# A new unit order for a one-core Sinkhorn-attention and gMLP kernel: V of the first batch mixed in 128 columns, narrow dummy matmuls ahead of P

## The chip, the core and the metric

The kernel runs on one core of a Trainium2 chip. The metric is device time in microseconds (us) of one execution, as the median of several runs. Before the change the median of five runs is 167.9 us (166.93 to 168.35).

The engines of the core are named as in the profile: PE is TensorE (PEld its weight loads), DVE is VectorE, ACT is ScalarE, POOL is GpSimd and SP is SyncE. Each works through its own instructions in program order, and semaphores order them against each other. DMAs are issued from two of these queues: SP issues the ones that move data between tiles, the transposing ones and the results; POOL issues the loads.

## What is computed

There are 4 batches (B), 8 heads (H), 768 positions (S) and 64 columns per head (D). A position belongs to one of 8 blocks of 96.

```
P = sort_net                                  # B, H, 8, 8
5 times: P = exp(P - rowmax); P /= rowsum; P /= colsum
k_sorted = P mixed over the 8 blocks of k     # and v_sorted likewise
attn     = softmax(q_block @ k_sorted_block.T / 8)   # inside each block of 96
x        = attn @ v_sorted_block              # B, S, 512
h = relu(x @ w_in)                            # 1024 columns: u = first half, v = second half
v_n = layer norm of v over its 512 columns
gated = u * (w_spatial @ v_n + b_spatial)     # w_spatial is 768 x 768
out = gated @ w_out
```

All matmuls take bf16 operands and sum in fp32.

## The kernel before

Its work is cut into units. A unit is a function `u_XY`, and the string `ORDER` is a list of calls, `XY:args`, that is run from first to last. There is no planner at run time: the place of a unit in `ORDER` is the place of each of its instructions on each engine and in each queue that it uses. Where an argument is a letter, it names the engine that empties PSUM or does the elementwise step (A for ACT, D for DVE, P for POOL). Where the first argument is a digit 0 to 7, it is the PSUM bank at which the unit's result starts; most units take two banks, and a unit whose banks are still being read waits on PE.

The units that the change and the prediction speak of:

- `LH`, `L`: one load each, issued by POOL (`L:k:2` loads k of batch 2; `L:wv`, `L:wu`, `L:ws`, `L:wo` the weights). q, k and v have two buffers each, so the load of batch 2 needs the buffer of batch 0.
- `SK`: one of five Sinkhorn rounds (ACT and DVE). `PR`: P spread by 8 small matmuls. `P0`: the mixing matrices of batch 0, in four parts on DVE. `PC`: a copy of the spread P, from which `PD` (POOL) makes the mixing matrices `pd` of the other batches.
- `DM:bank:n:w`: n dummy matmuls on a zeroed tile, w columns wide; nothing reads them.
- `QT`, `KT`: q turned, and k mixed and turned, for one pair of heads: 12 matmuls into two banks and one copy of 128x768. `QX`: for batches 2 and 3, q is turned by a DMA instead: two DVE copies (L180) and a transposing DMA on SP (L182).
- `VT` and `VX`, batch 0 only: v mixed and turned for one pair of heads (L338, then a copy), and turned back by 4 transposes per half of the blocks (L375), into `vb`. `VM` and `VC`, other batches: v mixed without turning (L387), then 4 DMAs per half (L402, SP) that regroup it into `vb`.
- `SC`: scores of one pair of heads and one half of the blocks (8 small matmuls, L420), and their exponential on ACT (`ex`, four buffers). `AT`: 8 small matmuls with `vb` (L445), and the division: on DVE, or, for the letter P, an ACT copy, a DVE reciprocal and a POOL product.
- `XT`: x of batch 0 turned on PE. `XX`: x of half a batch turned by a transposing DMA on SP (L189), for batches 1 to 3.
- `VP`: v half of the first layer, tiles of 128 positions, 4 matmuls of 512 columns each (L488), relu and statistics. `LN`: the reciprocal deviations (ACT). `LA`: normalising one tile (POOL L518 and L519, or DVE L522).
- `UP`: u half, 8 matmuls of 384 columns (L533). `WS`: w_spatial turned, 6 transposes. `BB`: the load of b_spatial.
- `SP`: the spatial product for 128 columns, 12 matmuls of 384 columns (L545), then `z` (DVE) and the gate `gt` (DVE or POOL). `OP`: two output tiles, 8 matmuls of 512 columns (L594), a copy and the store. `SH` and `OH` are their halves at the end of the last batch.
- `WT`: a one-element POOL copy of a tile that a transposing DMA writes. What POOL issues after it waits until that DMA has landed.

In the order before, the turned v of batch 0 is made in halves of 64 columns (8 `VT` units), and each half has a buffer of its own (tag `vT`, three buffers). k and q of batch 3 stand behind `WT:x:1:0`, and `QX:D:3` stands on DVE ahead of `LA:D:1:1` and `LA:D:1:3`.

Of the kernel before, what the change touches and what calls it, by code (L numbers as in the profile page):

```python
# [9 lines left out]
BF16 = mybir.dt.bfloat16  # L10
# [38 lines left out]


# [9 lines left out]
def kernel(  # L60
# [25 lines left out]
    HP = H // 2  # L86
# [7 lines left out]
    att = ctx.enter_context(tc.tile_pool(name="att", bufs=2))  # L94
# [49 lines left out]
    st = {}  # L144
# [190 lines left out]
    def mix_T(t, src, b, hp, lo, n):  # L335
        for g in range(G):
            for hh in range(2):
                nc.tensor.matmul(  # L338
                    t[hh * 64:hh * 64 + 64, g * n:(g + 1) * n],
                    lhsT=src[:, 2 * hp + hh, g * D:(g + 1) * D],  # L340
                    rhs=pd[b][:, 2 * hp + hh, lo:lo + n],
                    start=True, stop=True,
                )
# [12 lines left out]
    def u_VT(ps, eng, hp, ih):  # L356
        hp, ih = int(hp), int(ih)
        lo, n = (0, 128) if ih == 2 else (ih * 64, 64)
        t = ps_tile(ps).rearrange("p x c -> p (x c)")
        mix_T(t, st["v", 0], 0, hp, lo, n)  # L360
        vT = att.tile([128, n * G], BF16, name="vT", tag="vT", bufs=3)
        copy(
            eng,
            vT.rearrange("p (x g) -> p x g", g=G),
            t[:, 0:n * G].rearrange("p (g x) -> p x g", g=G),
        )
        for y in range(2):
            if ih in (y, 2):
                st["vT", hp, y] = vT[:, HW * y if ih == 2 else 0:][:, 0:HW]
# [272 lines left out]
```

## Time and profile before

| | |
|---|---|
| median of 5 runs | 167.9 us (166.93 to 168.35) |
| profiled execution: its time | 168.42 us |
| profiled execution: span, first to last instruction | 166.6 us |
| PE matmuls busy | 142.4 us, 85% of the span |
| DVE / ACT / POOL busy | 117.6 / 82.6 / 52.8 us |
| mean granted TensorE clock | 0.98 |
| mean DMA rate | 153 GB/s, 25.49 MB moved |

The profile is of one execution. The span leaves out 1.8 us of the execution's own time. The strips of the page cut the span into 40 slices of 4.17 us; a digit is the busy share of a slice in tenths, and PEclk is the clock that PE was granted. The list of waits says which engine and line stood idle, what ended the idle time, how many microseconds in all, how often, and the longest one. The chain of waits is followed back from the last instruction; each of its lines has a start, a length and what took the time.

### The profile page before, as it was taken

The page shows a single profiled execution, that of the slowest core. Times are in us where ns is not written, and L with a number is a line of the kernel's source. Part 1 is how long each engine was busy: PE and PEld are TensorE (multiplying, and loading weights), DVE is VectorE, ACT ScalarE, POOL GpSimd, SP SyncE. Part 2 cuts the span into 40 slices and gives each one's busy share as a digit, 9 for nine tenths or more (in the row PEclk, how much of TensorE's full clock was granted, in tenths as well). Part 3 has the DMA queues.
Part 4 walks back from the last instruction along what each step waited for, and adds up shares of the span by engine and source line. Part 5 has one row for each costly group of instructions (what it writes and reads, how often), then busy time and mean ns, then how long its engine had stood idle before and what let it go on. Part 6 is the DMA issues. An engine that isn't in the chain of part 4 may idle for free.

```text
span 166.6 us, 3795 instructions
## 1 busy us (share of the span) xinstructions
PE 142.4 (85%) x1545; PEld 86.9 (52%) x1559; DVE 117.6 (71%) x237; ACT 82.6 (50%) x127; POOL 52.8 (32%) x73
## 2 busy tenths in 40 slices
PE   0477888999999898999973599999999999999790
PEld 0345777565866754555541265654555655456330
DVE  3767868896986859867720864989967897409950
ACT  3323968576984923684881023436762406740011
POOL 7915950249424535162600040032104200200300
PEclk9999999999999999999999569999999999999999
DMA  2999999999999999979999995000383500053055
GB/s 21 160 195 204 207 210 207 204 204 206 203 256 260 201 144 168 213 123 119 241 252 178 263 244 99 0 0 29 114 208 130 94 0 0 35 213 134 0 191 189
DMA packets 36689, 25.49 MB, mean 153 GB/s; under 512 B 16576, under 2 KB 33472, under 8 KB 36672
## 3 DMA queue, kind: packets, MB, share of 16 engines
q0 software_dynamic: 14864, 12.19, 48.3%
q1 hardware_dynamic: 21808, 13.06, 33.0%
q8 instruction: 12, 0.20, 0.5%
q14 instruction: 5, 0.04, 0.1%
HBM read 24.78 MB, written 6.29 MB: 186 GB/s over the span
## 4 chain that ended last, share of the span: by engine, by line
PE 47%; DMA 30%; POOL 7%; DVE 6%; issue 4%; ACT 3%; SPq 1%; POOLq 0%; ACTq 0%; DVEq 0%
DMA v_in<-in_v_dram 15%; PE ps L545 11%; DMA q_in<-in_q_dram 11%; PE ps L488 9%; PE ps L533 8%; PE ps L594 6%; DMA vb<-vm 3%; PE ps L445 3%; PE ps L420 3%; PE ps L338 2%; DVE z L551 2%; POOL v_sb L519 2%; POOL k_in L155 2%; PE ps L375 1%; DMA out_dram<-oh_sb 1%
## 5 line engine op out<-in xcount | busy, mean ns | idle before, releaser
L545 PE MATMUL ps<-wspT,v_sb 128*128 128x384 bf16 x180 | 32.8, 337 | 4.1 <-DVE v_sb L522 4.1
L457 POOL TENSOR_TENSOR x_sb<-xr,rec 96x512 bf16<-96x512 f32 x13 | 13.4, 1039 | 49.4 <-DVE rec L456 49.4
L433 ACT ACTIVATE ex<-ps 96x768 bf16<-96x768 f32 x32 | 24.8, 804 | 7.9 <-PE ps L420 7.4
L545 PEld LDWEIGHTS <-v_sb 128*128 128x128 bf16 x180 | 17.5, 100 | 16.1 <-DVE v_sb L522 4.5
L533 PE MATMUL ps<-xT,w_in_sb 128*128 128x384 bf16 x128 | 23.6, 331 | 0.1
L488 PE MATMUL ps<-w_in_sb,xT 128*128 128x512 bf16 x88 | 21.9, 379 | 0.4
L551 DVE TENSOR_TENSOR z<-ps,b_bc 128x768 f32<-128x768 f32 x15 | 14.2, 954 | 10.8 <-PE ps L545 8.8
L502 DVE BATCH_NORM_STATS2 stats<-v_sb 128x6 f32<-128x512 bf16 x24 | 16.3, 679 | 3.6 <-ACT v_sb L113 3.1
L594 PE MATMUL ps<-w_out_sb,gt 128*128 128x512 bf16 x67 | 16.3, 379 | 0.5 <-issue 0.3
L533 PEld LDWEIGHTS <-w_in_sb 128*128 128x128 bf16 x128 | 12.2, 99 | 8.3 <-issue 0.5
L113 ACT ACTIVATE v_sb<-ps 128x1024 bf16<-128x1024 f32 (+1 forms) x8 | 7.3, 916 | 14.7 <-PE ps L488 10.8
L519 POOL TENSOR_SCALAR v_sb<-v_sb,nm,rstd 128x512 bf16<-128x512 bf16 x11 | 8.8, 796 | 16.7 <-issue 11.2
L453 ACT COPY xr<-ps 96x520 f32<-96x520 f32 x13 | 7.4, 586 | 13.1 <-PE ps L445 11.8
L488 PEld LDWEIGHTS <-xT 128*128 128x128 bf16 x96 | 8.9, 98 | 9.3
L445 PE MATMUL ps<-vb,ex 96*128 96x65 bf16 x256 | 12.7, 196 | 1.1 <-DMA vb<-vm 0.9
L457 DVE TENSOR_TENSOR x_sb<-ps,rec 96x512 bf16<-96x512 f32 x19 | 13.0, 687 | 0.7
L445 PEld LDWEIGHTS <-ex 96*128 96x128 bf16 x256 | 10.9, 99 | 4.3 <-issue 1.6
L113 ACT ACTIVATE u_sb<-ps 128x768 bf16<-128x768 f32 x12 | 9.7, 811 | 6.1 <-PE ps L533 5.8
L557 DVE TENSOR_TENSOR gt<-z,u_sb 128x768 bf16<-128x768 f32 x12 | 12.2, 1014 | 0.4
L323 PE MATMUL ps<-ident,q_in 128*64 128x128 bf16 x96 | 4.6, 243 | 7.7 <-DMA q_in<-in_q_dram 6.4
L107 ACT CAST vm<-ps 128x768 bf16<-128x768 f32 x10 | 7.8, 801 | 6.1 <-PE ps L387 6.0
L594 PEld LDWEIGHTS <-gt 128*128 128x128 bf16 x72 | 6.6, 98 | 7.3
(89 smaller groups left out, 207.0 us busy)
## 6 DMA issues: line engine op xcount, KB each, us to landing
out_dram<-o_sb SPq DMA_DIRECT2D x9, 512.0 KB, 4.2
k_in<-in_k_dram POOLq DMA_DIRECT2D x4, 768.0 KB, 13.8
v_in<-in_v_dram POOLq DMA_DIRECT2D x4, 768.0 KB, 12.1
vb<-vm SPq DMA_DIRECT2D x24, 99.0 KB, 7.5
q_in<-in_q_dram POOLq DMA_DIRECT2D x3, 768.0 KB, 20.1
out_dram<-oh_sb SPq DMA_DIRECT2D x6, 256.0 KB, 2.1
wsp_nat<-in_moe_w_spatial_dram POOLq DMA_DIRECT2D x1, 1152.0 KB, 21.5
w_in_sb<-in_moe_w_in_dram POOLq DMA_DIRECT2D x2, 512.0 KB, 15.9
```

Source lines behind the costliest of these rows:

```text
L113: nc.scalar.activation(out=out, in_=in_, func=AF.Relu)
L433: nc.scalar.activation(out=dst, in_=src, func=AF.Exp, scale=scale)
L445: nc.tensor.matmul(t[:, hh, ii * VW:ii * VW + D + 1], lhsT=e[:, c:c + 128], rhs=vb[b % 2][:, ih * NI + ii, 2 * hp + hh, 0:D + 1], start=Tr ...
L457: (nc.gpsimd if eng == "P" else nc.vector).tensor_mul(out=x_sb[:, hp].rearrange("p i (h d) -> p h i d", h=2), in0=tv[:, :, :, 0:D], in1=_r ...
L488: nc.tensor.matmul(t[:, x, :], lhsT=x_tile(b, n // 3)[:, kc, n % 3 * 128:(n % 3 + 1) * 128], rhs=w_in_sb[:, kc, DH:DFF], start=(kc == 0), ...
L502: nc.vector.bn_stats(out=stats, in_=v_sb[:, x, :])
L519: nc.gpsimd.tensor_scalar(out=v_sb, in0=v_sb, scalar1=nm[:, 0:1], scalar2=rs[:, n:n + 1], op0=ALU.add, op1=ALU.mult)
L533: nc.tensor.matmul(t[:, x, 0:HW], lhsT=w_in_sb[:, kc, mc * 128:(mc + 1) * 128], rhs=x_tile(b, ih)[:, kc], start=(kc == 0), stop=(kc == KC ...
L545: nc.tensor.matmul(t[:, x, 0:HW], lhsT=st["v_sb", b, n][:, mc * 128:(mc + 1) * 128], rhs=wspT[:, n, x * HW:(x + 1) * HW], start=(n == 0), ...
L551: nc.vector.tensor_add(out=z.rearrange("p (x c) -> p x c", x=2), in0=t[:, :, 0:HW], in1=b_bc.rearrange("p (x c) -> p x c", x=2),)
L557: eng.tensor_mul(out=gt, in0=z, in1=st["u", b, mc // 2][:, mc % 2])
L594: nc.tensor.matmul(t[:, x, :], lhsT=st["gt", b, mc][:, c * 128:(c + 1) * 128], rhs=w_out_sb[:, mc, :], start=(mc == 0), stop=(mc == FC - 1),)
```

## The change

Three things change. First, `VT` writes all 128 columns for a pair of heads at once (four units instead of eight), into one tile that holds all four pairs and takes the buffer of tag `qX`, which batches 2 and 3 use later for their turned q. Second, the dummies ahead of `PR` are four groups of 12 with 192 columns and one of 2 with 384, where they were two groups of 6 with 384; two single dummies later on are gone. Third, the whole `ORDER` is another one: other places, banks and engines for nearly all units. The number and kind of the other units is the same.

Parts of the new order that matter for what follows: five `PD` units stand between `L:wv` and `L:v:1`, three of them ahead of `L:ws`; `L:v:1`, `L:k:1`, `L:q:1` stand behind the POOL product of an `AT`; `L:v:3` comes before the attention of batch 1 instead of behind it; k and q of batch 3 stand behind `WT:q:2:0`; on SP, both transposes of x of batch 1 come before the one of q of batch 2, and the regrouping of v of batch 3 (`VC:3`) comes after `QX:D:3`; `QX:D:3` comes after two `SP` units of batch 1.

```diff
--- before.py
+++ after.py
@@ -14,37 +14,37 @@
 
 
 ORDER = """
-LH:q:0:0:4 IN SK:0 ID MK SK:0 SK:0 L:k:0:0:128 QT:0:A:0:1:2 SK:0 QT:2:A:0:0:2 DM:0:6:384 SX
-DM:2:6:384 SK:1 PR:0 L:v:0:0:128 P0:1:0:4 P0:0:0:4 P0:1:4:8 P0:0:4:8 DM:7:5:384 KT:2:D:0:1:2 PC:A
-KT:4:A:0:0:2 KT:0:D:0:2:2 VT:7:A:1:0 VT:6:A:3:0 IV:0 VT:2:D:0:0 LH:q:0:4:8 SC:4:0:0:1 VX:7:D:1:0 L:wv
-SC:0:0:1:0 VX:2:D:3:0 VT:6:D:0:1 L:wu L:ws QT:4:A:0:3:2 IV:1 VT:7:D:2:0 SC:0:0:0:0 VX:6:D:0:1
-AT:2:D:0:1:0 KT:4:A:0:3:2 QT:6:A:0:2:2 PD:1:4:8 VX:0:D:0:0 VX:1:D:2:0 SC:4:0:3:0 AT:2:D:0:0:1
-VT:0:A:1:1 L:v:1:0:128 VT:7:D:3:1 VT:1:A:2:1 AT:4:D:0:3:0 SC:2:0:2:0 AT:6:D:0:0:0 PD:3:4:8 VX:0:A:2:1
-L:k:1:0:128 DM:1:1:384 SC:4:0:1:1 AT:2:D:0:2:0 SC:0:0:2:1 VX:7:D:1:1 XT:6:A:0:0:0 VX:4:D:3:1
-XT:2:D:0:0:1 AT:0:D:0:2:1 SC:3:0:3:1 L:q:1:0:128 AT:6:D:0:1:1 PD:1:0:4 VP:2:A:0:2 PD:3:0:4 L:wo
-PD:2:0:4 AT:3:P:0:3:1 VP:0:D:0:0:1 XT:7:A:0:1:0 UP:3:A:0:0:0 XT:7:A:0:1:1 VM:0:D:1:1 WS:6:D:0
-WS:2:D:3 LN:0:0:3 LA:P:0:1 L:v:2:0:128 WS:3:D:1 VM:4:A:1:3 VP:7:A:0:5 VP:0:A:0:3:4 UP:2:A:0:0:1
-LA:P:0:2 VM:6:A:1:2 UP:0:D:0:1:1 LA:P:0:0 VM:2:A:1:0 VC:1:1 KT:6:D:1:0:2 KT:4:A:1:1:2 KT:0:A:1:3:2 BB
-QT:2:D:1:2:2 QT:6:A:1:0:2 L:k:2:0:128 LN:0:3:6 KT:4:D:1:2:2 QT:0:D:1:3:2 VC:1:0 QT:2:A:1:1:2 LA:D:0:4
-L:q:2:0:128 SC:6:1:0:1 UP:4:D:0:1:0 PD:2:4:8 SC:2:1:2:1 SC:0:1:3:1 WS:7:D:4 WS:6:D:5 VM:4:A:2:2
-LA:P:0:5 VM:2:D:2:3 WS:7:D:2 VM:0:A:2:1 LA:P:0:3 DM:6:1:384 SC:4:1:1:1 AT:2:D:1:0:1 AT:0:P:1:2:1
-SC:6:1:0:0 L:v:3:0:128 AT:4:D:1:1:1 AT:2:D:1:3:1 SP:0:P:0:3 SC:4:1:1:0 KT:6:A:2:0:2 KT:2:D:2:2:2
-SC:4:1:3:0 KT:0:D:2:3:2 AT:6:P:1:1:0 KT:2:D:2:1:2 SC:4:1:2:0 XX:1:1 AT:0:P:1:3:0 QX:D:2 SP:6:D:0:0
-AT:0:P:1:2:0 AT:2:D:1:0:0 XX:1:0 SP:4:P:0:1 VM:6:A:2:0 SP:0:D:0:2 VC:2:1 VM:2:A:3:1 VM:6:A:3:3
-VP:4:D:1:4:5 VM:6:A:3:2 VM:0:A:3:0 UP:2:D:1:0:1 SC:6:2:1:1 LN:1:4:6 SC:0:2:0:1 LA:P:1:4 VC:3:0
-WT:x:1:0 L:k:3:0:128 OP:4:D:0:2 L:q:3:0:128 SC:2:2:3:1 SC:6:2:2:1 UP:0:A:1:1:0 VC:2:0 AT:2:D:2:1:1
-AT:4:P:2:0:1 VP:6:D:1:0:1 AT:4:P:2:2:1 AT:2:P:2:3:1 VP:0:A:1:2:3 SC:2:2:1:0 SC:6:2:2:0 UP:4:A:1:1:1
-VC:3:1 XX:2:1 OP:0:D:0:0 LN:1:0:4 LA:P:1:0 SC:4:2:0:0 SC:6:2:3:0 UP:2:A:1:0:0 KT:0:A:3:2:2 LA:D:1:2
-LA:D:1:5 KT:6:A:3:3:2 QX:D:3 LA:D:1:1 LA:D:1:3 OP:4:D:0:1 AT:0:D:2:3:0 AT:6:P:2:2:0 SP:2:D:1:0
-AT:0:P:2:1:0 AT:4:D:2:0:0 UP:6:A:2:1:1 SP:2:D:1:2 VP:4:A:2:4:5 SC:2:3:2:1 SC:6:3:3:1 SP:0:D:1:3
-AT:2:P:3:2:1 SP:4:D:1:1 XX:2:0 KT:0:D:3:1:2 KT:2:A:3:0:2 UP:6:A:2:1:0 AT:2:D:3:3:1 VP:4:D:2:0:1
-SC:2:3:1:1 LN:2:4:6 LA:P:2:5 SC:6:3:1:0 OP:0:A:1:0 AT:2:D:3:1:1 LA:D:2:4 VP:4:D:2:2:3 SC:2:3:0:1
-SC:0:3:3:0 OP:6:A:1:2 AT:0:D:3:0:1 AT:2:D:3:1:0 LN:2:0:4 UP:4:D:2:0:0 UP:6:A:2:0:1 SC:2:3:2:0
-SC:0:3:0:0 LA:P:2:0 LA:D:2:3 LA:D:2:1 XX:3:1 LA:D:2:2 OP:4:D:1:1 AT:2:P:3:2:0 AT:6:P:3:3:0 SP:0:D:2:2
-AT:6:D:3:0:0 VP:4:A:3:4:5 UP:0:A:3:1:1 LN:3:4:6 SP:2:D:2:1 SP:0:D:2:3 XX:3:0 SP:2:D:2:0 VP:0:A:3:2:3
-VP:2:A:3:0:1 UP:0:A:3:0:0 UP:6:A:3:1:0 LA:D:3:4 LN:3:0:4 LA:D:3:3 LA:P:3:5 OP:0:A:2:0 LA:P:3:0
-LA:D:3:1 UP:6:A:3:0:1 LA:D:3:2 OP:2:A:2:2 OP:6:A:2:1 SP:2:D:3:0 SP:6:D:3:2 SP:2:P:3:1 SH:7:D:3:3:0
-SH:6:D:3:3:1 OH:7:D:3:1 OH:6:D:3:0 OH:2:A:3:4 OH:7:D:3:5 OH:6:D:3:2 OH:2:A:3:3
+IN LH:q:0:0:4 ID SK:0 MK SK:0 SK:0 QT:0:A:0:1:2 QT:2:D:0:0:2 DM:0:12:192 SK:0 L:k:0:0:128 SX
+DM:2:12:192 L:v:0:0:128 SK:1 DM:0:12:192 IV:0 DM:2:12:192 DM:7:2:384 PR:0 P0:1:4:8 P0:0:4:8 P0:1:0:4
+P0:0:0:4 PC:A DM:7:5:384 KT:2:A:0:2:2 KT:4:D:0:3:2 IV:1 KT:0:A:0:1:2 VT:6:D:1:2 KT:2:A:0:0:2
+LH:q:0:4:8 VT:4:D:0:2 SC:0:0:1:1 VX:7:D:1:0 L:wv SC:2:0:0:1 PD:3:4:8 L:wu VX:6:D:1:1 VT:0:D:3:2
+QT:4:A:0:2:2 PD:2:0:4 PD:1:4:8 QT:6:D:0:3:2 L:ws VT:2:A:2:2 PD:3:0:4 PD:2:4:8 VX:0:D:0:1 AT:4:P:0:1:1
+VX:1:D:3:0 SC:6:0:2:0 L:v:1:0:128 SC:2:0:2:1 VX:0:D:2:1 L:k:1:0:128 AT:4:D:0:0:1 VX:1:A:2:0 PD:1:0:4
+SC:6:0:3:1 VX:0:D:0:0 AT:2:D:0:2:1 AT:4:D:0:2:0 VX:1:A:3:1 SC:6:0:3:0 SC:2:0:1:0 L:q:1:0:128
+AT:0:D:0:3:1 AT:6:D:0:3:0 SC:4:0:0:0 AT:2:P:0:1:0 XT:0:A:0:1:1 XT:1:D:0:1:0 AT:6:P:0:0:0 XT:4:A:0:0:1
+WS:2:A:3 WS:3:D:0 VP:0:D:0:3:4 WS:7:A:1 XT:2:A:0:0:0 VP:3:D:0:5 VM:0:A:1:2 VM:6:A:1:3 VM:4:A:1:1
+VP:2:D:0:2 VM:0:A:1:0 LN:0:3:6 VP:6:A:0:0:1 VC:1:0 UP:0:A:0:1:0 KT:6:A:1:2:2 KT:4:A:1:1:2
+KT:2:D:1:3:2 UP:0:D:0:0:1 L:wo LA:P:0:3 LN:0:0:3 L:v:2:0:128 QT:6:A:1:3:2 LA:P:0:5 QT:2:D:1:1:2
+L:k:2:0:128 KT:4:A:1:0:2 QT:0:D:1:0:2 SC:6:1:3:0 WS:2:D:4 L:q:2:0:128 SC:4:1:3:1 LA:P:0:2
+QT:0:D:1:2:2 LA:D:0:4 SC:6:1:1:0 SC:2:1:0:0 WS:4:D:2 WS:5:D:5 L:v:3:0:128 AT:0:D:1:3:0 UP:6:A:0:1:1
+LA:P:0:0 VC:1:1 LA:P:0:1 SC:4:1:2:0 AT:2:D:1:0:0 AT:0:D:1:1:0 UP:6:A:0:0:0 AT:2:D:1:2:0 AT:4:D:1:3:1
+BB SP:0:D:0:3 SC:4:1:2:1 SC:2:1:0:1 SP:6:P:0:1 VM:2:A:2:1 KT:4:D:2:3:2 AT:0:P:1:2:1 XX:1:0 SC:6:1:1:1
+KT:2:A:2:0:2 AT:0:D:1:0:1 SP:4:D:0:2 AT:0:P:1:1:1 VM:2:A:2:2 SP:6:P:0:0 XX:1:1 VM:2:A:2:3 QX:D:2
+VM:4:A:2:0 VP:0:D:1:0:1 UP:4:A:1:0:0 VM:2:D:3:0 VC:2:0 VM:0:A:3:1 OP:6:D:0:2 KT:0:D:2:1:2 WT:q:2:0
+L:k:3:0:128 KT:2:A:2:2:2 VP:4:A:1:2:3 L:q:3:0:128 VM:0:A:3:3 UP:2:A:1:1:1 SC:4:2:3:0 VC:2:1
+SC:6:2:2:0 VP:0:D:1:4:5 SC:4:2:1:0 SC:2:2:0:0 UP:6:A:1:1:0 AT:0:D:2:3:0 LN:1:0:4 LN:1:4:6 LA:D:1:5
+AT:4:P:2:2:0 LA:P:1:2 LA:D:1:1 OP:2:A:0:0 LA:D:1:4 LA:D:1:0 LA:D:1:3 AT:6:P:2:1:0 AT:0:P:2:0:0
+OP:4:D:0:1 SC:6:2:1:1 XX:2:0 SC:2:2:2:1 UP:0:A:1:0:1 SC:4:2:0:1 SC:6:2:3:1 SP:2:D:1:3 AT:4:P:2:0:1
+SP:6:P:1:0 VM:2:A:3:2 QX:D:3 AT:4:P:2:2:1 SP:0:D:1:2 AT:4:P:2:3:1 AT:2:D:2:1:1 SP:6:P:1:1
+VP:0:A:2:0:1 KT:2:A:3:1:2 XX:2:1 UP:4:A:2:0:0 KT:0:A:3:2:2 KT:2:D:3:3:2 KT:6:A:3:0:2 VC:3:0
+OP:4:D:1:2 SC:6:3:0:0 SC:2:3:1:0 UP:0:A:2:1:1 SC:4:3:2:0 SC:6:3:1:1 VC:3:1 VP:2:A:2:2:3 AT:4:P:3:0:0
+VP:0:A:2:4:5 AT:2:P:3:1:0 UP:4:A:2:1:0 LN:2:0:4 OP:0:D:1:1 LA:D:2:3 LA:D:2:1 LN:2:4:6 SC:4:3:3:0
+SC:2:3:2:1 LA:D:2:2 OP:6:A:1:0 LA:P:2:4 LA:P:2:0 LA:D:2:5 AT:2:D:3:1:1 AT:0:P:3:2:0 UP:4:A:2:0:1
+AT:2:D:3:3:0 AT:0:D:3:2:1 SP:6:D:2:3 SC:2:3:3:1 SC:4:3:0:1 SP:0:D:2:1 AT:4:P:3:0:1 XX:3:0 SP:2:P:2:2
+AT:0:D:3:3:1 XX:3:1 UP:4:D:3:0:0 SP:2:D:2:0 VP:4:A:3:0:1 UP:2:A:3:1:0 OP:0:D:2:2 VP:2:A:3:2:3
+VP:0:A:3:4:5 LN:3:0:4 OP:2:A:2:0 LA:P:3:3 UP:0:D:3:0:1 LN:3:4:6 LA:P:3:1 LA:P:3:4 LA:D:3:0 LA:D:3:2
+LA:D:3:5 UP:4:A:3:1:1 OP:0:A:2:1 SP:4:D:3:1 SP:0:D:3:2 SP:4:P:3:0 SH:0:D:3:3:0 SH:1:D:3:3:1
+OH:0:A:3:1 OH:1:A:3:0 OH:4:A:3:4 OH:0:D:3:2 OH:1:A:3:3 OH:4:A:3:5
 """
 
 
@@ -358,7 +358,9 @@
         lo, n = (0, 128) if ih == 2 else (ih * 64, 64)
         t = ps_tile(ps).rearrange("p x c -> p (x c)")
         mix_T(t, st["v", 0], 0, hp, lo, n)
-        vT = att.tile([128, n * G], BF16, name="vT", tag="vT", bufs=3)
+        if "vT" not in st:
+            st["vT"] = att.tile([128, HP, S], BF16, name="vT", tag="qX", bufs=1)
+        vT = st["vT"][:, hp, lo * G:(lo + n) * G]
         copy(
             eng,
             vT.rearrange("p (x g) -> p x g", g=G),
```

## The prediction

> **What bounds the kernel now.** I read the strips first, then PE's waits, then the chain inside the stretch where the strips show a hole, then sums by stage.
>
> ```profile
> span 166.6 us, 3795 instructions
> PE   0477888999999898999973599999999999999790
> PEclk9999999999999999999999569999999999999999
> ```
>
> PE is at 9 nearly everywhere; that makes it the bound. There are three exceptions: the start, the end, and slices 20 to 22 (84 to 96 us), where its clock is also halved.
>
> ```profile
> PE ps L545 <- DVE v_sb L522: 4.1, 1, 4.1
> PE ps L338 <- DMA k_in<-in_k_dram: 1.3, 2, 0.9
> PE ps L323 <- issue: 1.3, 1, 1.3
> ...
> PE ps L445 <- DMA vb<-vm: 0.9, 2, 0.5
> ...
> PE ps L375 <- issue: 0.3, 1, 0.3
> ```
>
> The largest wait of PE after the start is for DVE's `LA`. The chain in that stretch says what DVE was doing:
>
> ```profile
> 73.74 18.32 DMA q_in<-in_q_dram
> ...
> 92.55 0.55 DVE qx L180
> 93.10 0.34 DVE v_sb L522
> 93.44 0.05 issue
> 93.49 3.38 PE ps L545 x10
> 96.87 0.88 PE ps L445 x16
> 97.75 1.74 PE ps L533 x8
> ```
>
> q of batch 3 is issued at 73.74 and takes 18.32 us. `QX:D:3` waits for it on DVE (7.6 us, in DVE's waits), and behind it stand the two `LA:D` that the `SP` unit then on PE needs. PE stops, and after the stop it runs at half clock: 10 matmuls in 3.38 us, where twelve take 1.95 us elsewhere. From 84.43 to 99.33, 14.9 us, PE does 24 pairs of `KT`, one `OP`, 4 `AT`, one `SP` and one `UP`, which at the undisturbed steps (0.71, 1.73, 0.98, 1.95, 1.30) is 6.7 to 6.8. **The hole costs 8.1 us**: 0.9 for k, 0.5 in small waits, 4.1 for `LA`, 2.6 for the clock.
>
> ```profile
> 16.00:42.00 26.00, 24.11 (x415) 17.60 (x411) 20.43 (x46) 19.46 (x30) 14.44 (x19) 1.00 1.26 206
> 42.00:84.00 42.00, 39.75 (x511) 25.11 (x509) 33.03 (x57) 28.20 (x45) 17.47 (x22) 1.00 1.18 194
> 84.00:100.00 16.00, 10.45 (x91) 5.93 (x91) 6.95 (x15) 4.35 (x7) 1.92 (x2) 0.79 1.13 233
> 100.00:156.00 56.00, 55.52 (x427) 31.32 (x432) 41.43 (x71) 24.28 (x36) 8.88 (x13) 1.00 0.28 78
> ```
>
> Columns: PE, PEld, DVE, ACT, POOL, clock, DMA share, GB/s. PE idles 1.9 us in the first row, 2.2 in the second, 0.5 in the last; DMA is saturated near 205 GB/s for the first 42 us.
>
> **The change, part by part.**
>
> *VT in 128 columns.* Eight units of 12 matmuls (steps 0.18 to 0.21 us, 1.5 in all) become four; a `KT` unit has the same shape and takes 0.34, so 1.4. Copies: four of DVE 0.552 and four of ACT 0.477 (4.1) become three of 0.947 and one of 0.801 (3.6). Gain below 0.5 us, on engines weighed below. Sharing the buffer with turned q costs nothing: its readers (`VX`) end near 27 us, its next user is `QX:D:2` near 61.
>
> *Start.* `QT:2` is now emptied by DVE, between two Sinkhorn rounds: p_t moves from 11.9 to 12.6. The dummies follow at 8.1: 384 columns took 0.32 us each until 9.7 and 0.162 after, so I take half of each for 192: 12 x 0.16, 36 x 0.081, 2 x 0.16 end at 13.3, and `PR` stands behind them (before, 11.99). Then four `P0` (1.4) and the copy: POOL and ACT get the spread P at 15.5 and not 14.25. v of batch 0 lands at 15.7 (4.23 + 11.43) as before, so PE's real start stays; only ACT begins late.
>
> *Instruction fetches.* PE's first gap without a cause comes after pair 223 of weight load and matmul, the second after 351: 128 pairs, 256 instructions. The queue of instructions moved 12 packets, 0.20 MB, so 16 KB each: the gaps are fetches. The page "Runtime: NRT & Kernel Launch" of the Trainium skill, section "Instruction fetch mechanics", has the same blocks of 256 but calls a crossing mostly hidden; by it this part is worth 0. The trace has 1.30 + 0.34 = 1.64 us. I follow the trace. The new order has 48 more pairs before v lands, so pair 223 falls in the last `VT` and 351 in `AT:2:P:0:1:0`, 7 us of PE work apart, where there were 5.6: I leave 0.3 of the 1.64.
>
> *What takes that gain.* Up to the last `XT` copy of batch 0, ACT now has 3 kT, 8 ex, qT, vT, 3 xT, 2 wspT (0.80 each), 3 xr (0.59) and 2 vb (0.57): 17.3 us, 15.5 to 32.8 without a pause. `VM` of batch 1 then needs v, which landed at 33.2 (15.38 + 17.8, the largest of v's landings). Its issue is now behind `PD`s and a POOL product that waits for an `AT`, so near 23 and not 15.4; but the loads ahead of it keep the queue full to 29, so it lands the same. Next on ACT: 4 vm, `LN`, v_sb, u, 2 kT, `LN`, qT, 8.4 us, to 42.0. So PE reaches `SC:6:1:3:0` at 42.1. Progress there, against before at 42.4: one `UP` less (1.30), one `KT` and three `QT` more (1.36). **Up to 42 us the gain is 0.3**, not 1.6.
>
> *42 to 90.* To the place of `QX:D:3` PE has 16 `SC`, 13 `AT`, 7 `SP`, 6 `UP`, 6 `VP` tiles, 3 `OP`, 8 `VM`, 4 `KT`, 1 `QT`, 3 `WS`: 42.9 us by the steps (0.25 to 0.31, 0.24, 1.95, 1.30, 0.865, 1.73, 0.33, 0.34). Before, 42.4 to 84.3 had 37.2 of such work in 41.9 us: 1.9 of named waits (0.6 v, 0.5 vb, 0.4 k, 0.3 z, in PE's waits of that stretch) and some 2.7 of slower steps. The slower steps stay. The named waits go: `vb` leaves at 37 and not 42, v of batch 3 is issued at 44 and not 52.7. A new one comes. In the order before, the one x transpose that was issued among loads is SP's at 53.32, and it is the longest of the landings of xT (the second row; the matmuls on it began at 66.1):
>
> ```profile
> 53.32 4.33 SPq L189 DMA_TRANSPOSE xT<-x_sb  x1
> ```
>
> ```profile
> DMA to landing us min/median/max: 3.8/5.0/12.7
> ```
>
> Now `XX:1:0` is issued near 51, with k, q and v still to come until 65.5. The Trainium skill, "DMA: Bandwidth & Descriptors", section "Queues, rings and completion order", says that a DMA engine takes the queues in turn, packet by packet; by equal turns it would share the loads' pace and land within 7 us, at 58, before `VP:0:D:1:0:1` wants it at 61.5: 0. By the row it lands at 63.7: **2.3 us** of wait. I take the row; ends 0 and 4 (behind the last load).
>
> *Is the hole gone?* SP: `XX:1:1` from 60.5 to 64, then q's transpose, 7.1 at most (the longest of qX): 71. `WT:q:2:0` on POOL holds k and q of batch 3 until then (before, issue at 72.8 and 73.7), and POOL's products for `AT` and a gate queue behind it, none wanted before 76. With the old 18.3 us q lands at 90.5; half of the 16 `vb` transfers that shared its time are now behind `QX:D:3`, so I estimate 87. `QX:D:3` is reached at 42.1 + 42.9 + 2.7 + 2.3 = 90. Behind it on DVE is no `LA` that PE wants at once: PE has two `AT`, one `SP`, two `AT` and one `SP` before it needs a bank that DVE must empty, 4.9 us. So q may land as late as 94 at no cost. If that cover fails, the price is the 8.1 again.
>
> *After 90.* 56.7 us of steps to `OH`; before, 55.9 took 56.5: 57.3. The end (`SP` gated by POOL, `SH`, six `OH`) has its old shape: 10.9. DVE's work per us is as before. **0**.
>
> *Sum against the profiled span*: 166.6 - 8.1 (hole) - 0.3 (to 42) - 1.9 (named waits) + 2.3 (xT) = 158.6; the 0.3 of fetch lies inside the second term. Counting forward: 90 + 57.3 + 10.9 = 158.2. With the 1.8 us around the span 160.3. The median lay 0.5 below the profiled run (167.9 against 168.42): 159.8, and with an estimate of 0.3 for small new waits **160.1**.
>
> **Rivals.**
> *A: nothing takes the gain* (transpose shares fairly, ACT isn't the bound). For: the rule above; ACT was busy only 19.46 of 26 us. Against: the 17.3 us counted. 160.1 - 2.3 - 1.6 = 156.2.
> *B: the hole comes back half.* q of batch 3 lands after 94, 3 us late, with part of the clock loss: 165. For: the load took 18 to 22 us three times. Against: fewer `vb` transfers beside it.
> *C: no change*: the old hole in full, elsewhere: 160.1 + 8.1 = 168.
> *D: slower.* Both x transposes of batch 1 now stand on SP ahead of the one of q of batch 2. If each crawls for 12.7 us, one behind the other, from 51 to 76.4, q's ends at 83.5, and `SC:4:2:3:0` (place 73.5) stops PE for 10 us, longer than the 4.1 after which the clock was halved: 2.6 more. 160.1 + 12.6 = 172.7. What follows shifts alike (gate, k and q of batch 3, `QX:D:3`). It decides, that is reaches 167.9, once q's transpose lands after 78.7 (73.5 + 7.8 - 2.6). Against: the loads end at 65.5, after which x transposes took 3.8 to 5.5.
>
> **How the numbers follow.** Forecast (157.5 to 164): 0.57. A: 0.11. B: 0.13. C: 0.06. D: 0.13. A measurement tells 0.5% (0.84 us) from no change. Faster: forecast, A, B: 0.81. Same: most of C, 0.05. Slower: D and the rest of C, 0.14. The range leaves out D, the upper edge of C and the lower half of A, about 0.2 in all: 156.0 to 168.2.
>
> **What would show it.** No wait of `SP` for `LA` or of qx for q above 1 us, and PEclk at 9 throughout: the hole. No gap without a cause above 0.5 us before 30 us: fetches. ACT busy above 90% from 16 to 33 and `VM` of batch 1 starting at 33 to 34: the bound early. A wait of L488 near 61 to 64: the transpose. The gate near 71, q landing before 94. Wrong would be: a PE gap above 3 us anywhere after 40, or a start of `SC:6:1:3:0` later than 44.

## The result, and the profile after

| | before | after |
|---|---|---|
| median | 167.66 us (166.21 to 171.34, 43 runs) | 166.63 us (165.78 to 169.05, 24 runs) |
| ratio, 95% interval | | 0.995 (0.993 to 0.997) |
| span of the profiled execution | 166.6 us | 164.6 us |
| mean granted TensorE clock | 0.98 | 0.98 |

The change is worth 1.0 us, where 7.8 had been forecast (167.9 to 160.1). Ratios here compare executions of the same rounds and leave disturbed ones out, so they need not be the quotients of the medians beside them.

The strips of the kernel after, in slices of 4.1 us, with the DMA rate below the clock:

```profile
span 164.6 us, 3766 instructions
PE   0499898499999998299999999999999999999780
PEclk9999999689999999789999999999999999999998
GB/s 18 166 190 204 176 162 198 203 204 204 217 222 260 203 196 147 166 187 120 165 270 243 217 16 143 155 235 88 52 205 97 24 71 127 61 110 88 0 254 132
```

The hole at 84 to 96 us is gone. In its place are two new ones, in slices 7 and 16 (counted from 0), each with a low clock of its own. In slices 4 and 5 the DMA rate is 176 and 162 where it was 207 and 210 before: the queue of loads ran thin. The rates of before:

```profile
GB/s 21 160 195 204 207 210 207 204 204 206 203 256 260 201 144 168 213 123 119 241 252 178 263 244 99 0 0 29 114 208 130 94 0 0 35 213 134 0 191 189
```

PE's waits in the kernel after (total us, how often, longest), and the group of the spatial product from the page:

```profile
PE ps L490 <- DMA xT<-x_sb: 4.0, 1, 4.0
PE ps L296 <- DMA wsp_nat<-in_moe_w_spatial_dram: 1.9, 1, 1.9
...
PE ps L338 <- issue: 0.6, 1, 0.6
```

```profile
L547 PE MATMUL ps<-wspT,v_sb 128*128 128x384 bf16 x180 | 31.4, 326 | 0.0
```

The spatial product (L545 before) had waited 4.1 us for `LA`, and its 180 matmuls had taken 32.8 us. Now it waits 0.0 and they take 31.4. What PE waits for instead are two transfers: w_spatial for `WS`, and the turned x of batch 1 for `VP:0:D:1:0:1`. The chain of waits says where these begin:

```profile
15.71 1.10 POOL pd L280
16.80 0.76 POOL w_in_sb L206
...
17.58 2.09 POOL pd L280 x2
19.67 11.10 DMA wsp_nat<-in_moe_w_spatial_dram
...
30.82 1.46 PE ps L296 x12
...
53.99 14.60 DMA xT<-x_sb
68.59 0.45 issue
69.04 2.84 PE ps L490 x7
```

`L:ws` is issued at 19.67, behind three `PD` products on POOL (7.57 before, ahead of all of them). It lands at 30.8 (29.0 before). The transpose takes 14.6 us, and the two `VP` tiles on it (8 matmuls, of which the trace has seven) take 2.84 us where two tiles take 1.73 elsewhere. Both stops are followed by half clock. The sums of two stretches (the last columns are clock, DMA share and GB/s):

```profile
30.44:33.85 3.41, 2.81 (x16) 1.93 (x18) 0.56 (x1) 0.80 (x1) 1.22 (x2) 0.50 1.31 204
67.99:71.40 3.41, 2.36 (x6) 1.02 (x8) 0.00 (x0) 0.00 (x0) 0.00 (x0) 0.50 1.12 221
```

By stage, in the columns and stretches shown of before:

```profile
16.00:42.00 26.00, 22.58 (x359) 16.55 (x356) 18.31 (x38) 20.06 (x31) 16.14 (x19) 0.93 1.23 192
42.00:84.00 42.00, 37.70 (x452) 23.45 (x449) 30.62 (x50) 23.59 (x34) 14.00 (x18) 0.96 1.18 192
84.00:100.00 16.00, 15.95 (x171) 9.85 (x170) 12.51 (x24) 10.09 (x18) 8.22 (x8) 1.00 0.70 161
100.00:156.00 56.00, 54.51 (x435) 30.45 (x441) 40.35 (x70) 27.12 (x40) 15.08 (x19) 1.00 0.45 107
```

PE gains 5.5 us of busy time in the third row (10.45 to 15.95). It loses 1.5 in the first (24.11 to 22.58) and 2.1 in the second (39.75 to 37.70), and of what is left, 2.8 and 2.4 us run at half clock. The places of PE, in us, show it as a sum:

| place on PE | forecast | measured | what the difference is |
|---|---|---|---|
| `PR:0` | 13.3 | 13.34 | |
| `SC:6:1:3:0` | 42.1 | 45.69 | +3.6: 1.9 w_spatial, 1.5 half clock (3.03 us of work after the stop, at half speed), the rest fetch |
| PE idle before `VP:0:D:1:0:1` | 61.5 | 65.09 | 0: 19.4 us of work in both |
| `VP:0:D:1:0:1` | 63.7 | 69.04 | +1.65: the stop is 3.95 and not 2.3 |
| place of `QX:D:3` | 90 | 95.37 | 0: 1.2 more by half clock, 1.2 less by steps |
| first `OH` | 147.3 | 154.34 | +1.7: 58.97 and not 57.3 |
| end of the span | 158.2 | 164.6 | -0.6: 10.3 and not 10.9 |

### The profile page after: what moved, and what is told of

It reads as the page before. It is cut to its first block, busy times and chain, and to the rows that moved or that the text cites. A ratio compares the mean times of both kernels' runs of the same rounds, so it can differ in the third digit from the quotient of the medians.

```text
span 164.6 us, 3766 instructions
## 1 busy us (share of the span) xinstructions
PE 143.6 (87%) x1536; PEld 89.7 (55%) x1547; DVE 112.9 (69%) x224; ACT 87.3 (53%) x133; POOL 59.8 (36%) x78
## 3 DMA queue, kind: packets, MB, share of 16 engines
q1 hardware_dynamic: 21808, 13.06, 33.6%
## 4 chain that ended last, share of the span: by engine, by line
PE 49%; DMA 24%; DVE 9%; issue 8%; POOL 4%; ACT 2%; POOLq 1%; DVEq 0%; ACTq 0%
DMA xT<-x_sb 12%; PE ps L490 12%; PE ps L535 10%; DMA wsp_nat<-in_moe_w_spatial_dram 7%; PE ps L547 7%; PE ps L596 5%; PE ps L289 3%; DMA q_in<-in_q_dram 3%; PE ps L447 3%; PE ps L422 3%; POOL pd L280 2%; PE ps L582 2%; DVE stats L504 2%; PE ps L296 2%; DMA vb<-vm 1%
## 5 line engine op out<-in xcount | busy, mean ns | idle before, releaser
L547 PE MATMUL ps<-wspT,v_sb 128*128 128x384 bf16 x180 | 31.4, 326 | 0.0
L459 POOL TENSOR_TENSOR x_sb<-xr,rec 96x512 bf16<-96x512 f32 x15 | 15.6, 1043 | 39.3 <-DVE rec L458 28.0
L490 PE MATMUL ps<-w_in_sb,xT 128*128 128x512 bf16 x90 | 23.9, 403 | 4.5 <-DMA xT<-x_sb 4.0
L547 PEld LDWEIGHTS <-v_sb 128*128 128x128 bf16 x180 | 16.9, 98 | 10.7
L559 POOL TENSOR_TENSOR gt<-z,u_sb 128x768 bf16<-128x768 f32 x6 | 10.4, 1736 | 19.2 <-DVE z L553 19.2
L113 ACT ACTIVATE u_sb<-ps 128x768 bf16<-128x768 f32 x13 | 10.5, 811 | 11.4 <-PE ps L535 11.0
L113 ACT ACTIVATE v_sb<-ps 128x1024 bf16<-128x1024 f32 x8 | 8.2, 1024 | 13.1 <-PE ps L490 13.0
L447 PE MATMUL ps<-vb,ex 96*128 96x65 bf16 x256 | 11.9, 193 | 0.5 <-issue 0.3
L459 DVE TENSOR_TENSOR x_sb<-ps,rec 96x512 bf16<-96x512 f32 x17 | 11.7, 687 | 0.8 <-DVE rec L458 0.2
L455 ACT COPY xr<-ps 96x520 f32<-96x520 f32 x15 | 8.7, 587 | 6.1 <-PE ps L447 3.0
L115 DVE TENSOR_SCALAR v_sb<-ps 128x1024 bf16<-128x1024 f32 (+1 forms) x5 | 5.0, 1001 | 7.4 <-PE ps L490 7.4
## 6 DMA issues: line engine op xcount, KB each, us to landing
k_in<-in_k_dram POOLq DMA_DIRECT2D x4, 768.0 KB, 12.7
q_in<-in_q_dram POOLq DMA_DIRECT2D x3, 768.0 KB, 15.9
```

Source lines behind the costliest of these rows:

```text
L113: nc.scalar.activation(out=out, in_=in_, func=AF.Relu)
L447: nc.tensor.matmul(t[:, hh, ii * VW:ii * VW + D + 1], lhsT=e[:, c:c + 128], rhs=vb[b % 2][:, ih * NI + ii, 2 * hp + hh, 0:D + 1], start=Tr ...
L459: (nc.gpsimd if eng == "P" else nc.vector).tensor_mul(out=x_sb[:, hp].rearrange("p i (h d) -> p h i d", h=2), in0=tv[:, :, :, 0:D], in1=_r ...
L490: nc.tensor.matmul(t[:, x, :], lhsT=x_tile(b, n // 3)[:, kc, n % 3 * 128:(n % 3 + 1) * 128], rhs=w_in_sb[:, kc, DH:DFF], start=(kc == 0), ...
L547: nc.tensor.matmul(t[:, x, 0:HW], lhsT=st["v_sb", b, n][:, mc * 128:(mc + 1) * 128], rhs=wspT[:, n, x * HW:(x + 1) * HW], start=(n == 0), ...
L559: eng.tensor_mul(out=gt, in0=z, in1=st["u", b, mc // 2][:, mc % 2])
```

## Experiments

All edits are to `ORDER`. "-" and "+" are units taken out and put in, at the place that the line names.

### Loads of the weights ahead of the `PD` products

```diff
 after:  ... VX:7:D:1:0 L:wv
+L:wu L:ws
 SC:2:0:0:1 PD:3:4:8
-L:wu
 ... QT:6:D:0:3:2
-L:ws
```

> Edit: in the changed kernel the loads of the u half of w_in and of w_spatial are issued directly behind the v half, ahead of POOL's products for the mixing matrices. Theory (two new waits took the gain; the first is w_spatial, issued late because POOL's products stand ahead of it): w_spatial lands near 29 and not at 30.8, the wait of 1.9 us ahead of WS goes, with it the first half-clock window of 3.4 us, and every later load lands about 1.5 us earlier. The wait for the transposed x stays, since it ends with the last load: time about 163.5 to 165 (1.5 to 3 us less than the changed kernel's 166.6). Rival (ACT bounds the early part, as the forecast had it): no gain, 166.6, and PE starts the scores of batch 1 at 45.7 as before.

Measured: 163.85 us (162.38 to 164.85), ratio 0.989 (0.984 to 0.995), span 160.6. The clock row of its strips, and PE's waits:

```profile
PEclk9999999999999999999999999999999999999998
```

```profile
PE ps L489 <- DMA xT<-x_sb: 1.8, 1, 1.8
PE ps L337 <- DMA k_in<-in_k_dram: 1.1, 1, 1.1
PE ps L337 <- issue: 0.9, 1, 0.9
```

POOL issued w_spatial at 7.83; it landed at 28.95, and no `WS` waits. `SC:6:1:3:0` starts at 43.65, 2.0 us earlier, although this execution lost more to a fetch (0.9) and started `PR` 1.3 later. The wait for x fell to 1.8 and cost no clock. So the late issue of w_spatial is a cause, worth 2.8 us by the medians (166.63 to 163.85). The ratio says less: 0.989 is what three of these executions give against the two quickest of before's 33 (165.63 and 166.05); by the medians it is 0.977. That ACT alone holds PE in this stretch is refuted: ACT executes the same work, and PE came forward. The later loads gained less than expected: those of batch 1 land 0.65 us earlier and not 1.5, those of batch 2 no earlier.

### v of batch 3 behind the first x transpose

The last load ahead of the transpose is moved behind it, so that the transpose has less beside it.

```diff
 after:
-L:v:3:0:128      (behind WS:5:D:5)
 ... XX:1:1 VM:2:A:2:3
+WT:x:1:0 L:v:3:0:128
-VM:2:D:3:0  VM:0:A:3:1
 ... UP:2:A:1:1:1
+VM:0:D:3:0
 SC:4:2:3:0 VC:2:1 SC:6:2:2:0
+VM:2:A:3:1
```

> Edit: in the changed kernel the load of v of batch 3 is held by POOL until the first transpose of x of batch 1 has landed, and the mixing of two of its head pairs is moved behind the matmuls that follow. Theory (the transpose crawls while loads are in the queue and lands only when the last of them has): with one load fewer in the queue it lands near 64 to 65 and not at 68.6, the wait of 4.0 us at the first VP of batch 1 falls below 1 us and the second half-clock window goes: 5 us less at that place; k, q of batch 3 come up to 4 us later, which costs 0 to 2: 161.5 to 164. Rival (the transpose needs 12 to 15 us in itself once issued): it still lands near 68, and v of batch 3 then comes late as well: 167 to 170.

Measured: 174.48 us (173.67 to 177.95), ratio 1.05 (1.043 to 1.058): slower, and by more than either theory or rival had. One wait of PE, and the piece of the chain behind it:

```profile
PE ps L388 <- DMA v_in<-in_v_dram: 10.8, 1, 10.8
```

```profile
68.10 15.46 DMA v_in<-in_v_dram
```

The edit did at its place what it was made for: the loads ahead end at 62.7, x lands at 63.6, and PE does not wait for it. But POOL came to the gate only at 67.6, behind a product for `AT` and a gate product of its own, so v was issued at 68.1, and q's transpose of batch 2 at 68.17. The two then took 15.5 and 15.6 us side by side, with six transfers for `vb` and a store beside them from 72 on. Between 72 and 89 us PE was busy 6.15 of 17 at a mean clock of 0.60. The loser of a collision was changed, not its price.

### `QX:D:3` later, in the kernel before

```diff
 before:  ... KT:6:A:3:3:2
-QX:D:3
 ... AT:0:P:2:1:0 AT:4:D:2:0:0
+QX:D:3
```

> Edit: in the kernel before, the two DVE copies and the transposing DMA of q of batch 3 are moved behind two divisions and the SP unit that stood behind them; nothing else. Theory (the hole of 8.1 us came from DVE standing at these copies with the normalising of v behind them): the hole and the half clock at 84 to 97 us go; the transposed q is then 2 to 3 us late for the scores of batch 3: 161 to 164 against 167.7. Rival (another wait stands right behind it, so the hole was not worth its 8.1 us): 166 to 168.

Measured: 166.40 us (164.43 to 170.22, 20 runs), ratio 0.993 (0.989 to 0.997), span 164.6; the rival's 166 to 168 holds. PE's waits:

```profile
PE ps L419 <- DMA qX<-qx: 2.7, 1, 2.7
PE ps L532 <- DMA xT<-x_sb: 1.7, 1, 1.7
...
PE ps L444 <- DMA vb<-vm: 1.3, 4, 0.6
```

And two lines of SP's transposes, from the chain:

```profile
86.23 6.95 DMA xT<-x_sb
...
95.27 5.72 DMA qX<-qx
```

The wait for `LA` and the half clock are gone, and only about 1.4 of the 8.1 us come out in the median (2.0 in the span). PE now stands for two other transfers. The first x of batch 2 lands at 93.2, as in the kernel before (93.4), where PE had no need of it yet, since it stood for `LA`. q of batch 3 still lands at 91.9, and the turned q at 101.0 (98.6 before); 2 us of that are the edit's own, since DVE comes to the copies at 93.9. **The hole was late transfers, of q above all, and `LA` was only the first victim.** In the new order q lands at 90.8, ahead of its place at 95.4, and the hole has nothing to come from.

### Dummies inside the two stops

```diff
 after:
+DM:2:12:384
 WS:2:A:3
 ...
+DM:0:24:384
 VP:0:D:1:0:1
```

> Edit: in the changed kernel 12 dummies of 384 columns stand ahead of the first WS and 24 ahead of the first VP of batch 1, where PE waits 1.9 and 4.0 us; nothing reads them. Theory (each of the two waits costs more than its length because PE's clock is halved for 3.4 us after it): the clock stays full, VP of 2 tiles takes 1.73 us and not 2.50 and 2.87, and the time falls by 1.5 to 2.5 us: 164 to 165.2. Rival (the half-clock work is hidden, because loads and transposes set the next starts anyway): 166.6 to 167.5.

Measured: 164.83 us (163.79 to 165.45, 14 runs), ratio 0.985 (0.981 to 0.989), mean clock 0.99. PE's waits:

```profile
PE ps L295 <- DMA wsp_nat<-in_moe_w_spatial_dram: 0.5, 1, 0.5
PE ps L337 <- issue: 0.5, 1, 0.5
PE ps L489 <- DMA xT<-x_sb: 0.4, 1, 0.4
```

The stops are as long as before, but PE works on dummies in them: w_spatial lands at 31.1 and the last load at 68.0. The clock stays, and 1.8 us come back. That is the price of the half clock apart from the stops; counted from the two stretches above it was 1.5 + 1.2. (The medians are compared here; by the ratios it is 1.7.)

### x of batch 1 turned on PE

With the loads first, one or both transposing DMAs are replaced by `XT`: for each half two units, 16 transposes and two copies in all.

```diff
 after, with L:wu L:ws behind L:wv:
 ... SP:6:P:0:1
+XT:0:A:1:0:0 XT:1:D:1:0:1
-XX:1:0
 (second kernel also)
-XX:1:1
 VP:0:D:1:0:1
+XT:6:A:1:1:0 XT:7:A:1:1:1
```

> Edit: the loads are issued first as in the run with early loads, and of batch 1 the first half of x is turned by 16 small matmuls and two copies instead of the first transposing DMA. Theory (a transposing DMA and loads in flight at the same time slow each other, and the transpose ends only with the loads): the wait of 1.8 us at the first VP of batch 1 and the 1.1 us for k go, q of batch 2 and v of batch 3 land 1.5 to 3 us earlier; cost 0.7 us of PE: 160.5 to 162.5 against 163.9 for early loads alone. Rival (the loads take their time with or without it): v of batch 3 lands at 68 as before, PE waits for it instead of for x: 163.5 to 165.

> Edit: as the run before it, and the second half of x of batch 1 on PE too, so that q of batch 2 is the first transposing DMA. Theory: q's transpose is issued near 61 and lands before 69, k and q of batch 3 start 3 us earlier; another 0.7 us of PE: 160.5 to 162.5, the same as the run before it or 1 us less. Rival (PE and ACT work is what is dear by now): 1 to 2 us more than the run before it.

Measured: 160.60 us (159.71 to 161.95), ratio 0.956 (0.948 to 0.964), for one, and 160.24 us (159.29 to 161.42), ratio 0.955 (0.949 to 0.960), for both. A second series of the latter gave 160.60 (159.67 to 161.04), ratio 0.960 (0.956 to 0.963). **It beats both kernels: it is 6.5 to 7.9 us below the one before in the same series, and about 6 below the one after.** Its strips:

```profile
span 157.5 us, 3830 instructions
PE   0399989999999999989999989999999999999790
PEclk9999999999999999999999999999999999999999
```

PE's waits with one transpose replaced, apart from those of the start:

```profile
PE ps L489 <- DVE z L552: 1.7, 1, 1.7
PE ps L581 <- POOL gt L558: 0.8, 1, 0.8
PE ps L295 <- DMA wsp_nat<-in_moe_w_spatial_dram: 0.6, 1, 0.6
```

The wait for k is gone, and of that for x 0.3 is left. The loads gain too. From the landing of k of batch 2 to that of v of batch 3, two loads later, it takes 7.8 us (54.6 to 62.4) without the transpose and 10.7 (57.4 to 68.0) with it. `XX:1:0` carried 0.39 MB (13.06 to 12.67 MB on the hardware queue of the page). It delayed the loads by 2.9 us and itself took 13.65 us to land; `XX:1:1`, issued here at 62.83 behind the last load, took 4.0.

The wait for z that remains is q of batch 3 again. It lands at 93.4, 4.7 us after the place of `QX:D:3` (88.8). With both replaced it is 92.1 against 88.6, 3.5 us late, and that wait is 0.6. The forecast had 4 us of cover there; by these two rows it is about 3 (4.7 - 1.7 and 3.5 - 0.6).

### The two named parts alone, in the order of before

```diff
 before, dummies:
-DM:0:6:384      +DM:0:12:192
-DM:2:6:384      +DM:2:12:192 DM:0:12:192 DM:2:12:192 DM:7:2:384
 before, V in 128 columns (with the new tile of u_VT):
-VT:7:A:1:0 VT:6:A:3:0      +VT:6:A:1:2 VT:2:D:3:2
-VT:2:D:0:0 VT:0:A:1:1 VT:7:D:3:1 VT:1:A:2:1
-VT:6:D:0:1      +VT:6:D:0:2
-VT:7:D:2:0      +VT:2:A:2:2
```

> Edit: in the kernel before, only the dummies ahead of P are those of the change (four times 12 with 192 columns, two with 384, instead of two times 6 with 384). Theory (the gaps without a cause come each 128 pairs of weight load and matmul, and a block is asked for when PE's queue crosses into the one ahead): 38 more pairs ahead of the first load move the first gap forward, to the scores near 18.5 us, and make it longer: 1.5 to 2.5 us in place of 1.3, so the dummies cost 0.3 to 1 us. Rival (the fetch is asked for earlier by as much as the dummies run earlier): a gap of at most 1.3 us.

> Edit: in the kernel before, only V of batch 0 is mixed in 128 columns (four VT units in place of eight, the tile of the change), places otherwise kept. Theory: PE's VT work is the same within 0.2 us, copies 0.5 us less, 48 pairs fewer ahead of the second fetch: 0 to 0.7 us less than the kernel before, the first gap comes 24 to 36 pairs of work later and is shorter. Rival (the wider copy makes the following VX wait): up to 1.5 us more, seen as waits of L377 for the copy.

Measured, one execution each: 171.80 us (span 170.0) with the dummies and 168.75 (span 166.7) with V in 128 columns, beside a median of 168.09 (167.22 to 169.19) of before. PE's waits with the dummies, and one line of those with V:

```profile
PE ps L544 <- DVE v_sb L521: 3.9, 1, 3.9
...
PE ps L419 <- issue: 1.2, 1, 1.2
PE ps L288 <- issue: 1.0, 1, 1.0
```

```profile
PE ps L545 <- DVE v_sb L522: 3.8, 1, 3.8
```

Neither shows a gain alone, and both keep the hole; the run with V in 128 columns lies within the range of before, so a small effect of it is open. The dummies push `PR` from 11.99 to 14.50 and the first `VT` from 15.70 to 17.11, and the two fetch gaps are 1.2 and 1.0, no less in sum than the 1.3 and 0.3 of before (the first is what the rival said: at most 1.3). That run also has three pieces of half clock of 3.41 us where before has two. In the new order the same dummies end at 13.3, and `VT` starts near 16. What gain there is belongs to the order, as far as is known: the run below takes the narrow dummies out of the new order at no loss, but V in 64 columns in the new order was not run.

### Old dummies in the best version

```diff
 best version (loads first, both x on PE):
-DM:0:12:192      +DM:0:6:384
-DM:2:12:192      +DM:2:6:384
-DM:0:12:192 DM:2:12:192 DM:7:2:384
```

> The version with the loads first and both x transposes on PE, with the dummies of before (two groups of 6 with 384 columns) in place of the narrow ones: 38 pairs of weight load and matmul fewer ahead of PR. Theory (a block of 128 pairs is fetched in 2.3 us from the start of its packet, and PE stands still for what its remaining pairs do not cover, whatever the dummies are): PR starts 0.5 to 1.3 us earlier, v still sets the start at 15.7; the block border moves 38 pairs later in the real work, near 22.5 us, with a gap of 0.5 to 1.3; the median within 0.6 us of the version with narrow dummies. Rival (the narrow dummies are what saves the fetch time, as the words of the change have it): gaps of 1.3 and 0.3 as before, 1 us slower.

Beside it, on the same chip, the version itself:

> The version with the loads first and both x transposes of batch 1 on PE, once more, as the measure for the two runs beside it: 159.5 to 161, about 0.955 of before.

Measured: 160.36 us (159.59 to 163.21), ratio 0.958 (0.954 to 0.962), with the old dummies; 160.60, ratio 0.960 (0.956 to 0.963), with the narrow ones. The rival (1 us slower) is out; the gap is 0.34, less than the 0.5 to 1.3 expected. The trace of each kernel has the start of the packet that brings the second block of instructions, and the start of the weight load after pair 223 ("gap" is PEld's idle time before it):

| kernel | packet starts | pair after it starts | gap |
|---|---|---|---|
| before | 19.24 | 21.56 | 1.41 |
| before, narrow dummies | 19.23 | 21.57 | 1.27 |
| after | 18.23 | 20.54 | 0.74 |
| after, loads first | 19.71 | 22.09 | 0.97 |
| best version, first series | 18.50 | 20.80 | 0.52 |
| best version, second series | 19.45 | 21.89 | 1.77 |
| best version, old dummies | 19.65 | 22.07 | 0.34 |

From packet to work it is 2.3 to 2.4 us in every row. PE stands still for what its remaining pairs don't cover. The start of the packet moves by 1.5 us over these rows, and by 1.0 between two executions of one program, whose gaps are 0.52 and 1.77. With 38 pairs fewer ahead PE arrives at the border later and so waits less: old dummies, latest packet but one, smallest gap.

### q of batch 3, by its place and by its load

```diff
 best version, first edit:
 ... SP:6:P:1:0 VM:2:A:3:2
-QX:D:3
 AT:4:P:2:2:1 SP:0:D:1:2
+QX:D:3
 best version, second edit:
 WT:q:2:0
+L:q:3:0:128
 L:k:3:0:128 ... VP:4:A:1:2:3
-L:q:3:0:128
```

> The version with the loads first and both x transposes on PE, with QX:D:3 one SP unit later on DVE (behind SP:0:D:1:2). In that version q of batch 3 lands at 92.1, 3.5 us after the place of QX:D:3, and the z of SP:0:D:1:2 stands behind it: VP:0:A:2:0:1 takes 0.9 us more than its two tiles need. Theory (the cover of QX:D:3 is about 4 us, and q is late by about that): these 0.9 us go, span 156.6, 0.5 us faster in the median. Rival (the late q only moves the wait: qX now lands later and SC:6:3:0:0, near 101, waits for it): no change, and PE waits 0.5 to 1 us for qX.

> The version with the loads first and both x transposes of batch 1 on PE, with the loads of batch 3 exchanged: q is issued ahead of k. In that version q lands at 92 to 94, 3.5 to 4 us after the place of QX:D:3, and VP:0:A:2:0:1 takes 0.8 to 0.9 us too long. Theory (only the lateness of q costs there; k is not wanted before KT:2:A:3:1:2, near 96): q lands near 85, QX:D:3 does not wait, k lands near 92, and PE reaches KT:2:A:3:1:2 about 1 us earlier: span 156.5 to 158, ratio 0.95 to 0.957. Rival (whichever of the two is second lands too late, as k did in the kernel before): KT waits for k by 1 us or more, and the ratio stays at 0.96.

Measured for the first: 160.61 us (159.96 to 161.54), ratio 0.962 (0.958 to 0.965), no change. A wait has moved, and not quite where the rival said:

```profile
PE ps L534 <- DMA xT<-x_sb: 1.4, 1, 1.4
```

Not the turned q is late but x of batch 2, which SP issues behind it.

Measured for the second: 160.76 us (158.58 to 162.72), ratio 0.949 (0.943 to 0.956; 0.958 by the medians), span 157.3. The waits of PE no longer name either load; all that is left, after the start, is the gate at the end and short ones:

```profile
PE ps L581 <- POOL gt L558: 0.8, 1, 0.8
PE ps L337 <- issue: 0.4, 1, 0.4
PE ps L489 <- DMA xT<-x_sb: 0.3, 1, 0.3
```

q lands at 85.1 and k at 92.6, before `KT` at 95.9. That the late q was what cost time there is shown. The gain is 0.6 to 0.8 us from the place of `QX:D:3` to the first `OH` (59.17 against 59.72 and 59.92). Its six runs spread over 4 us, so whether the median gains is open.

## Why the prediction was wrong

**What held.** The hole went, for the reason given: q of batch 3 landed at 90.8, before its place on DVE, and no `SP` waits for `LA`. Some of that is luck: PE came to this place 5.4 us later than forecast. In the best version, where it comes at 88.6, q is 3.5 us late, and the order's cover keeps the cost at 0.6. `PR` started at 13.34 (13.3), and from 42.1 to 61.5 the sum of PE's steps met the measured 19.4 us. q's gate on POOL released k at 73.9 and not 71, since the x transposes ahead of q's were late. Both signs that the prediction had named for being wrong appeared: a PE gap above 3 us after 40 (3.95), and `SC:6:1:3:0` later than 44 (45.69).

**The step that failed first** is "but the loads ahead of it keep the queue full to 29, so it lands the same", under "What takes that gain". That step counted the late issue of v of batch 1. It left out that two of the loads ahead, `L:wu` and `L:ws`, are moved behind the same `PD` products. The sum for ACT has two `wspT` copies in it, which cannot begin before w_spatial lands, but no term for that landing. The rate fell to 162 GB/s, w_spatial landed 1.7 us later than before while PE reached `WS` sooner, and v landed at 34.6 and not 33.2. The stop for w_spatial and the half clock behind it are 3.4 of the 3.6 us lost by `SC:6:1:3:0`. The first of the experiments shows it.

**"Up to 42 us the gain is 0.3"** rested on ACT as the bound. Its duration was counted well: ACT was busy 91% from 15.9 to 28.8, when PE stopped for w_spatial. With no wait left, in the best version, PE reaches `SC:6:1:3:0` at 42.45, close to 42.1. But PE is then busy 24.99 of the 26 us from 16 to 42, and ACT 23.27: PE is the bound there, and the agreement is a coincidence.

**The wait for x**, "By the row it lands at 63.7: 2.3 us", had the right mechanism and the wrong size. The transpose took 14.6 us where the row had 12.7, and was issued 3 us later than counted. The stop was 3.95. By the equal turns of the Trainium skill ("DMA: Bandwidth & Descriptors", "Queues, rings and completion order") it would have been 0: the row was nearer and still too kind.

**The clock was left out of the new wait.** The prediction charged the old hole 2.6 us for half clock and the new stop nothing, with "longer than the 4.1 after which the clock was halved" as the point from which it would cost. Stops of 3.95 and 1.87 were followed by it, and 2.7 us of the loss are theirs (1.8 by the dummies).

**Fetches.** "I leave 0.3 of the 1.64" was 0.74 + 0.24 in the profiled execution. The Trainium skill ("Runtime: NRT & Kernel Launch", "Instruction fetch mechanics") calls a crossing mostly hidden; the trace of before spoke against it, and so does the table above, with gaps of 0.34 to 1.77. But the reason given, where the borders fall in the order, is only half of it. The other half is when the packet starts. That differed by 1.0 us between two executions of one program, so the order does not settle it.

**After 90.** 57.3 was 58.97. Against the 56.7 of steps, the spatial products took 1.1 more (0.8 is the gate, which falls ahead of the first `OH`, where the forecast had it in the tail), `SC` 0.45, `UP` 0.3, `KT` 0.2, and the rest is smaller; the eleven `AT` took their 0.24. The forecast had allowed 0.6 for such steps.

Of the rivals, the hole's return (B, C) and a late q of batch 2 (D) did not come. B (165) and C (168) came near in size, C as the case of no change, but by another mechanism: the hole was neither halved nor moved, two other transfers took its gain.

## What to carry to other kernels

When a reordering moves an elementwise unit ahead of a load in the same queue, write down the new issue time of **every** load behind it, and set its landing against the time at which its first user is reached in the new order. A hole that is cured by order is worth no more than the next-latest transfer allows: here 8.1 us of hole gave 1.0, and about 7 once two other transfers were put right. A transposing DMA that is issued among a queue of loads is slow and slows them; a few transposes on a PE that would stand still for it are the cheaper way.

## What the runs showed of the hardware that was not expected

- A transposing DMA and loads from DRAM in flight together slow each other. An x transpose among the loads took 13.65 us, and 4.0 behind the last one; two loads took 10.7 us beside it and 7.8 without, 2.9 us for the 0.39 MB of the transpose, while a load of 768 KB costs 3.9. With q's transpose (15.6) and v (15.5) side by side the transfers for `vb` shared the time, so that pair does not show it alone.
- Half clock came in pieces of 3.41 us, one after each of two stops (1.87 and 3.95), two after the hole of before. Yet stops of 2.66 (`QX:D:3` later, in the kernel before) and 1.75 (loads first) cost none, and with V in 128 columns in the order of before one piece came at 26.1 us, with no stop above 0.7 in the 8 us ahead of it. The length of a stop alone doesn't decide; from 26 to 28 us, just ahead of the stop of 1.87, PE was busy 1.60. What does decide isn't settled.
- The packet that brings the second block of instructions starts anywhere from 17.9 to 19.7 us, and the work it carries begins 2.3 to 2.4 us later in 13 of the 14 traces. In the other (V in 128 columns, order of before) PE comes to the border 3.2 us after the packet's start, and there is no gap.
